# Seven products in place of eight: a second Strassen stage in a fused FNet and SwiGLU kernel on Trainium2

## The chip, the cores and the metric

The kernel runs on one core of one Trainium2 chip, in one launch. The metric is the device time of that launch in microseconds (us), as a median of several executions. The profile shows one further execution. Five engines matter here: TensorE (PE in the profile, PEld for its weight loads), VectorE (DVE), ScalarE (ACT), GpSimd (POOL) and SyncE (SP). In this kernel SP and POOL mostly issue transfers (DMAs).

## The reference

The input is x, 2048 tokens of 512 numbers, fp32. A condition vector gives six modulation vectors; between them stand two sublayers, a Fourier mixing and a gated feed-forward of width F = 1792.

```python
mod = (_silu(c) @ w_mod).reshape(c.shape[0], 6, 1, -1)
sa, ca, ga, sb, cb, gb = (mod[:, 0], mod[:, 1], mod[:, 2], mod[:, 3], mod[:, 4], mod[:, 5])
h = _layernorm(x) * (1 + ca) + sa
a = jnp.einsum("bsd,ed->bse", h, dft_hid_re)
b = jnp.einsum("bsd,ed->bse", h, dft_hid_im)
y = jnp.einsum("ts,bse->bte", dft_seq_re, a) - jnp.einsum("ts,bse->bte", dft_seq_im, b)
x = x + ga * y
h = _layernorm(x) * (1 + cb) + sb
gate, up = h @ w1, h @ w3          # 512 -> 1792, twice
x = x + gb * ((_silu(gate) * up) @ w2)   # 1792 -> 512
```

## The kernel before

**Tiles.** A tile has 128 partitions. Tokens lie in four blocks t of 512, the 512 features in four chunks d of 128, and F in seven groups g of 256, each of two chunks q of 128. Big tiles come from 50 slots of [128, 2, 512] fp32, handed out first in, first out (`take`, `give`). A slot that is taken again makes the new writer wait for the last readers of the old tile. PSUM has eight banks of [128, 512] fp32.

**Precision.** Every fp32 product is three matmul passes in a faster format (`product`, L98 to L106): high part by high part, high by low, low by high. ScalarE makes the high part of an operand by a copy (`copy`, L87), VectorE the low part by a subtraction (`minus`, L90). So each operand of TensorE costs these two engines one pass each, the low after the high.

**Stages.** First come the norm, its modulation and the DFT over features; then the DFT over the sequence (`seq_unit`, L750); then the second norm (`ln2`), whose first blocks 0 and 2 begin when half of the sequence products are done; then the feed-forward. The feed-forward works on two pairs of token blocks, PAIRS = ((0, 2), (1, 3)). For the first pair the groups g = 0 and 1 are plain: `up_block` forms gate and up of one block and chunk in 12 matmuls each, `down_unit` one product with w2 in 6. Then come 12 *items*, each a group g and a pair: g = 2 to 6 of the first pair, then g = 0 to 6 of the second. `turning` = 5 is the first item of the second pair.

**An item.** Its products with w1 are the units a1 to a7, those with w3 the units b1 to b7 (`factor`). They are the seven products of Strassen's method (in Winograd's form) over a 2 x 2 split of the weights and of the operand, whose other side is the two token blocks. A unit is 6 matmuls. Their sums are built with copies by ScalarE (n = 1, 5, 6) and additions by VectorE (n = 2, 3, 7); `result` then puts silu on the w1 side and multiplies with the w3 side, which gives h, a tile v; its high and low part are `hf`. The products with w2 are 8 second products y for a pair (two blocks by four feature chunks), 6 matmuls each, so an item has 14 + 8 = 22 units. They run one item late: those of an item stand among the units of the next. ScalarE copies each result from the bank, scaled by gb (`copy_by`, L335); after two of them GpSimd issues a transfer that adds the y tile (512 KB) to `sums[t, i]` in DRAM (L1146). For the second pair and g = 5 and 6, VectorE adds into SBUF instead (`own`).

**What sets the order.** Each engine runs its own instructions in the order in which the program writes them. The units' order is the string `body` with `head` in the main loop; a minus sign marks units of the item before. Beside the units runs work from two queues, `background` (modulation columns, residual additions, second norm) and `jobs` (weights): `advance` takes steps from them while there is credit of VectorE and ScalarE time, with a rule for free slots, and stops at a `PAUSE`. `behind(n, fn)` puts a piece of work n units later. The steps of a weight (`weight_jobs`) are: high parts, four sums over its quarters, low parts, and high and low parts of the sums.

**Other parts that the change touches.** `mod_columns` forms the modulation vectors ga, sb, cb and gb: w_mod's columns by silu(c) (`times`), then two `tensor_reduce`. `add_sums` adds the last quarter of the sequence products to the blocks 1 and 3 (VectorE, L808); these steps stand at the end of `background`. `judge` forms a flag from sums of squares that were taken on the way, with which the kernel tells whether its shortcuts hold for the DFT matrices given; some 15 small operations of VectorE. The flag chooses at the very end between ending and another program (`general`), which doesn't run here.

Of the kernel before, what the change touches and what calls it, by code (L numbers as in the profile page):

```python
# [15 lines left out]
P = 128  # L16
# [26 lines left out]
def folded(nc, pools, c, cp, wmr, wmc, x, xt, ctr, cti, wdr, wdi, w1, w3, w2, out):  # L43
# [300 lines left out]
    def mod_columns(v, dst):  # L344
        w = {}

        def fetch(i):
            w[i] = take(F32, "wmc")
            nc.sync.dma_start(w[i], wmc[v, i])

        def scale(i):
            times(w[i], w[i], sc_row[0][:, 0, :].unsqueeze(1).to_broadcast([P, 2, N]))

        def total(i):
            r1 = small.tile([P, 32], F32, name=f"r1_{v}_{i}", tag="r1")
            nc.vector.tensor_reduce(
                out=r1,
                in_=flat(w[i]).rearrange("p (a b) -> p a b", b=32),
                axis=AX.X,
                op=OP.add,  # L360
            )
            nc.vector.tensor_reduce(
                out=dst[:, 2 * i : 2 * i + 2],
                in_=r1.rearrange("p (a b) -> p a b", b=16),
                axis=AX.X,
                op=OP.add,
            )
            give(w[i])
# [12 lines left out]
        background.extend([PAUSE] * 2)  # L381
        for i in range(2):
            step(background, 0, lambda i=i: scale(i), 1.2)
            step(background, 0, lambda i=i: total(i), 1.3)
        step(background, 0, end, 0.1)
# [689 lines left out]

    def up_block(g, t, q, w):
        if q == 0 and w == "w1":
            drain(lambda: ("h2", t, 1) in done)
        to = bank(turn[0] % 4)
        turn[0] += 1  # L1080
        for d in range(ND):
            at = slice(d * P, (d + 1) * P)
            product(
                to,
                [u[:, q, at] for u in wuse[w, g]],
                [u[t, d // 2][:, d % 2, :] for u in (h2h, h2l)],
                d == 0,
                d == ND - 1,
            )
        if t == PAIRS[0][1] and q == 1:  # L1090
            give_w((w, g))
# [117 lines left out]
    state, vs = {}, {}  # L1209

    def right(pair, n):
        t0, t1 = PAIRS[pair]
# [6 lines left out]
    def result(i, w, q, k, src):  # L1219
# [16 lines left out]
        behind(1, highs)  # L1236
        behind(2, lows)

    def factor(i, w, n):
# [37 lines left out]
        if n == 3:  # L1277
# [3 lines left out]
            if w == "w3":  # L1281
                for x in vs.pop(i):
                    behind(3, lambda x=x: give(x))

# [269 lines left out]
    give(zz)  # L1554

    USED = {"w1": (0.0, 0.5), "w3": (1.2, 0.5), "y": (0.0, 0.6), "own": (0.7, 0.0)}
# [6 lines left out]

    def beside(us, used):
        advance(us - used[0], us - used[1], jobs)
        if not jobs:
            advance(0.0, 0.0)

    def up(g, t):
        for q in range(2):
            for w in ("w1", "w3"):
                drain(lambda: ((w, g), "l") in done, jobs)
                delayed()
                up_block(g, t, q, w)
                beside(2.72, USED[w])

    def down(g, pair, t, d, key):
        drain(lambda: (key, "l") in done, jobs)  # L1580
        delayed()
        down_unit(g, pair, t, d, key)
        beside(1.36, USED["own" if pair == 1 and g >= NG - 2 else "y"])
# [36 lines left out]

    def unit(kind, i, n):
        g, pair = items[i]
# [13 lines left out]
        if (kind, n) == ("a", 6):  # L1636
            load_w(("w2", g, pair))
        if (kind, n) == ("a", 3) and more:
            load_w(("w3", *items[i + 1]))
            weight_jobs(i + 1, "w1")  # L1640
        if (kind, n) == ("b", 2):
            plain_jobs(("w2", g, pair))
        if (kind, n) == ("b", 3):
# [5 lines left out]
            if i + 1 == turning:  # L1649
                other_operands()  # L1650
            if more:
                weight_jobs(i + 1, "w3")
            for t in PAIRS[pair]:
                seconds.extend((g, pair, t, d, ("w2", g, pair)) for d in range(ND))
        beside(1.36, FACTOR[kind][n])

    weight_jobs(0, "w3")
    ln2(1)
    ln2(3)
    for i in range(len(items)):  # L1660
        body = "a6 a5 y a7 y y a4 y a3 y b1 y b2 y b6 b5 y"
        if i == turning:
            body = "y y y y y a6 y a5 y a7 y b1 b2 a4 b6 a3 b5"
        if i == len(items) - 1:
            body = "a6 a5 y a7 y y a4 y a3 b1 y b2 b6 b5 y b7 y b4 y b3 y y y y y y y y"
        head = "-b7 a1 -b4 -b3 a2 " if i == turning else "-b7 a1 a2 -b4 -b3 " if i else "a1 a2 "
        for at in (head + body).split():
            if at == "y":
# [3 lines left out]
            elif at[0] == "-":  # L1672
                unit(at[1], i - 1, int(at[2]))
            else:
                unit(at[0], i, int(at[1]))
    while later:
# [803 lines left out]
```

## Time and profile before

| | |
|---|---|
| time, median of 3 runs | 710.24 us (709.85 to 710.78) |
| profiled execution, its own time | 708.46 us |
| its span from the first to the last instruction | 706.7 us |
| mean granted TensorE clock | 0.991 |
| sequence products | 88 to 262 us |
| plain groups of the first pair, with the second norm | 262 to about 320 us |
| items of the first pair, then of the second | to about 503 us, then to the end |
| HBM read, written | 76.81 MB, 33.55 MB |

The page gives busy times per engine over the whole span, so a share there is a mean over stages with different limits. Groups of instructions stand as line, engine, operation, destination <- source with their shapes, count, busy time and mean ns; an idle time in brackets is what the engine waited just before an instruction, and for whom. TensorE's matmuls are pipelined: one lasts about 390 ns, and they start about 230 ns apart.

### The profile page before, as it was taken

The numbers are of one execution on the slowest core, as the hardware profiler recorded it, in microseconds if no ns is written. First come the engines' busy times: TensorE is split into PE (matmuls) and PEld (weight loads), VectorE is DVE, ScalarE is ACT, GpSimd is POOL, SyncE is SP. The second block draws the span as 40 slices with busy tenths as digits, with TensorE's granted clock in tenths as the row PEclk, the third lists the DMA queues.
The fourth block names the chain that finished last, engine by engine and source line by source line (L and its number), as shares of the span: only waits on it lengthen the run. The fifth ranks groups of instructions, "written<-read, shape, count | busy, mean of one in ns | idle before, by whom it ended". The sixth has DMA issues, their size and how long they took to land.

```text
span 706.7 us, 8912 instructions
## 1 busy us (share of the span) xinstructions
PE 686.3 (97%) x3152; PEld 564.7 (80%) x3152; DVE 548.3 (78%) x877; ACT 430.8 (61%) x709; POOL 119.4 (17%) x141
## 2 busy tenths in 40 slices
PE   7999999999999999899999999999999999999995
PEld 4898888888888888687888788787788888888784
DVE  5999679997999978579987886896865556664763
ACT  4998865545454655745677676867665565656420
POOL 1320253542524000200100101011010100101000
PEclk9999999999999999999999999999999999999998
DMA  8730299796678521522868558376763847537403
GB/s 266 211 120 1 77 373 328 251 307 229 207 283 287 168 86 41 92 58 64 209 114 199 89 130 153 61 156 137 239 136 73 180 62 175 111 69 162 137 0 124
DMA packets 38100, 108.93 MB, mean 154 GB/s; under 512 B 4896, under 2 KB 5152, under 8 KB 38048
## 3 DMA queue, kind: packets, MB, share of 16 engines
q0 software_dynamic: 12352, 43.00, 29.3%
q1 hardware_dynamic: 25264, 63.98, 27.5%
q10 hardware_dynamic: 432, 1.31, 0.5%
q8 instruction: 26, 0.43, 0.3%
q14 instruction: 26, 0.21, 0.1%
HBM read 76.81 MB, written 33.55 MB: 156 GB/s over the span
## 4 chain that ended last, share of the span: by engine, by line
PE 81%; DVE 7%; ACT 6%; issue 2%; DMA 2%; SPq 1%; ACTq 0%; DVEq 0%
PE bank L100 52%; PE bank L750 25%; PE bank L559 2%; PE bank L598 1%; DMA wmr<-in_wmr 1%; ACT xc L894 1%; PE bank L576 1%; DVE xc L96 1%; SPq L231 1%; ACT hf L87 1%; ACT y L335 1%; DVE v L96 0%; DVE hl L90 0%; ACT hm L501 0%; DMA w<-in_wdi 0%
## 5 line engine op out<-in xcount | busy, mean ns | idle before, releaser
L100 PE MATMUL bank<-hf,w2h 128*128 128x512 f32 (+1 forms) x452 | 140.9, 391 | 0.3
L1146 POOL DMA_DIRECT2D sum<-y x48 | 41.0, 855 | 390.1 <-ACT y L335 373.0
L100 PEld LDWEIGHTS bank<-hf,w2h 128*128 128x128 f32 x452 | 84.3, 188 | 22.1 <-DVE hf L90 3.4
L100 PE MATMUL bank<-hf,w2l 128*128 128x512 f32 (+1 forms) x226 | 87.6, 388 | 0.0
L87 ACT ACTIVATE hf<-v 128x512 fp32r<-128x512 f32 x56 | 35.3, 630 | 67.3 <-DVE v L96 62.7
L335 ACT ACTIVATE y<-bank,gb 128x512 f32<-128x512 f32 x96 | 64.9, 682 | 18.6 <-PE bank L100 18.3
L93 DVE TENSOR_TENSOR v<-bank,x 128x512 f32<-128x512 f32 x36 | 24.7, 685 | 34.9 <-PE bank L100 34.8
L750 PE MATMUL bank<-bh,us 128*128 128x512 f32 x128 | 49.9, 390 | 0.0
L93 DVE TENSOR_TENSOR x<-bank,x 128x512 f32<-128x512 f32 x36 | 24.7, 687 | 32.4 <-PE bank L100 28.7
L750 PE MATMUL bank<-bh,ul 128*128 128x512 f32 x128 | 49.8, 389 | 0.0
L750 PE MATMUL bank<-d,us 128*128 128x512 f32 x128 | 49.8, 389 | 0.0
L750 PE MATMUL bank<-d,uh 128*128 128x512 f32 x128 | 49.8, 389 | 0.0
L750 PE MATMUL bank<-l,us 128*128 128x512 f32 x128 | 49.8, 389 | 0.0
L750 PE MATMUL bank<-l,uh 128*128 128x512 f32 x128 | 49.8, 389 | 0.0
L100 PEld LDWEIGHTS bank<-hf,w2l 128*128 128x128 f32 x226 | 42.4, 188 | 8.4
L90 DVE TENSOR_TENSOR hf<-v,hf 128x512 fp32r<-128x512 f32 x56 | 38.5, 687 | 12.2 <-ACT hf L87 12.1
L170 POOL DMA_INDIRECT re<-in_ctr,mirror x32 | 35.8, 1117 | 66.2 <-DVE ul L90 39.5
L1224 ACT ACTIVATE v<-v 128x512 f32<-128x512 f32 x36 | 22.8, 632 | 38.8 <-DVE v L93 38.8
L87 ACT ACTIVATE x<-bank 128x512 f32<-128x512 f32 x72 | 41.4, 586 | 7.2 <-PE bank L100 6.5
L170 POOL DMA_INDIRECT im<-in_cti,mirror x32 | 32.7, 1023 | 35.3 <-PE bank L750 10.0
L100 PE MATMUL bank<-h2h,w1h 128*128 128x512 f32 x80 | 31.8, 397 | 1.5 <-ACT h2h L87 1.5
L100 PE MATMUL bank<-h2l,w1h 128*128 128x512 f32 x80 | 31.9, 399 | 0.8 <-DVE h2l L90 0.8
(246 smaller groups left out, 1775.2 us busy)
## 6 DMA issues: line engine op xcount, KB each, us to landing
sum<-y POOLq DMA_DIRECT2D x48, 512.0 KB, 5.6
w<-in_w SPq DMA_DIRECT2D x42, 512.0 KB, 4.5
re<-in_ctr SPq DMA_DIRECT2D x32, 256.0 KB, 5.0
im<-in_cti SPq DMA_DIRECT2D x32, 256.0 KB, 5.0
wmc<-in_wmc SPq DMA_DIRECT2D x8, 512.0 KB, 6.3
xr<-in_xt SPq DMA_DIRECT2D x8, 512.0 KB, 7.6
sum<-xr SPq DMA_DIRECT2D x8, 512.0 KB, 6.2
x<-in_x SPq DMA_DIRECT2D x11, 256.0 KB, 4.8
```

Source lines behind the costliest of these rows:

```text
L87: nc.scalar.activation(dst, src, AF.Copy, scale=scale)
L90: nc.vector.tensor_tensor(out=dst, in0=a, in1=b, op=OP.subtract)
L93: nc.vector.tensor_tensor(out=dst, in0=a, in1=b, op=OP.add)
L96: nc.vector.tensor_tensor(out=dst, in0=a, in1=b, op=OP.mult)
L100: nc.tensor.matmul(acc, lhs[a], rhs[b], start=first and n == 0, stop=last and n == len(PASSES) - 1, skip_group_check=more,)
L170: nc.gpsimd.indirect_dma_start(dst, None, rows, bass.IndirectOffsetOnAxis(ap=at, axis=0))
L231: queue.dma_start(raw_w[dt][q * 64 : (q + 1) * 64, m, :], w[i][par::2, q])
L335: nc.scalar.activation(dst, src, AF.Identity, scale=by)
L559: nc.tensor.matmul(halves(hb[k])[:, m, :], sides((hh, hl)[a][k])[:, dt, m, :], wu[dt][:, b, m, :], start=False, stop=dt % 2 == 1 and n == ...
L750: nc.tensor.matmul(acc[what, e], lhs, rhs, start=begin and i == 0, stop=(end or (turn and what == "x")) and i == len(terms) - 1, skip_grou ...
L1146: nc.gpsimd.dma_start(sums[t, d // 2], y, accum_op=OP.add)
L1224: behind(k != 0 or q == 0, lambda: nc.scalar.activation(v, src, AF.Silu))
```

## The change

The second products of the second pair's items with g = 0 to 4 (`SEVEN`, five items) become seven products M1 to M7 each in place of eight. The split is 2 x 2 over the two chunks q of h and the two token blocks on one side, and over the quarters of w2 on the other. VectorE forms four combinations of h's quarters and of w2's; these and their high and low parts are new operands (`seven_parts`, `seven_jobs`). The products run in the order 2, 5, 3, 1, 6, 7, 4, each on both banks 6 and 7 (two output chunks, 3 + 3 matmuls). M2, M5 and M1 begin new banks; the others add to what the banks hold (M3 to M5's, M6, M7 and M4 to M1's). After each product ScalarE copies both banks, which stay held, and GpSimd adds the y tile to `sums` of one block and half; the sums come out right because each output block gets copies of the partial sums that belong to it. So there are seven accumulating transfers an item in place of four.

```diff
+    SEVEN = [(g, 1) for g in range(NG - 2)]
+    ORDER7 = (2, 5, 3, 1, 6, 7, 4)
+    LEFT7 = {1: "h0", 2: "h2", 4: "h3", 5: "s0", 6: "s1", 7: "s2", 3: "s3"}
+    TO7 = {2: (0, 0), 5: (1, 1), 3: (0, 1), 1: (0, 0), 6: (0, 1), 7: (1, 1), 4: (1, 0)}
...
         times(v, v, src)
+        if (g, pair) in SEVEN:
+            seven_parts(i, q, k)
+            return
...
+    def seven_parts(i, q, k):
...
+        if (q, k) != (0, 1):
+            n = {(0, 0): 1, (1, 0): 2, (1, 1): 3}[q, k]
+            behind(1, lambda: high(n, v[q, k]))
+            behind(2, lambda: low(n, v[q, k]))
+            return
+        t1, t2, t3, t4 = v[0, 0], v[1, 1], v[0, 1], v[1, 0]
+        behind(1, lambda: minus(t1, v[0, 1], v[0, 0]))
+        behind(2, lambda: high(5, t1))
+        behind(2, lambda: minus(t3, v[1, 1], v[0, 1]))
+        behind(3, lambda: low(5, t1))
+        behind(3, lambda: minus(t2, v[1, 1], t1))
+        behind(4, lambda: high(7, t3))
+        behind(4, lambda: minus(t4, v[1, 0], t2))
+        behind(5, lambda: high(6, t2))
+        behind(5, lambda: low(7, t3))
+        behind(6, lambda: high(4, t4))
+        behind(7, lambda: low(6, t2))
+        behind(8, lambda: low(4, t4))
...
+    def seven_unit(g, pair, n, key):
+        new = n in (1, 2, 5)
+        if new:
+            banks7[:] = [bank(6), bank(7)]
+        y = take(F32, "y")
...
+        for e, to in enumerate(banks7):
+            at = int(LEFT7[n][1]) * HALF + e * P
+            product(
...
+            copy_by(y[:, e, :], to, gb[:, d : d + 1])
+        give(u)
+        nc.gpsimd.dma_start(sums[t, which], y, accum_op=OP.add)
+        behind(4, lambda: give(y))
```

`seven_jobs` has the five steps of `weight_jobs`, for w2. The order of units after such an item changes, ScalarE gets no step from the queues in a unit ahead of a y (`hold`), and the next item's w3 steps are queued at b6 in place of b3:

```diff
+        if i and items[i - 1] in SEVEN:
+            body = "a6 a5 a7 y a4 y a3 y b1 y b2 y b6 y b5 y"
...
-    def beside(us, used):
-        advance(us - used[0], us - used[1], jobs)
+    def beside(us, used, hold=False):
+        if hold:
+            credit[1] = min(credit[1], 0.0)
+        advance(us - used[0], 0.0 if hold else us - used[1], jobs)
...
+            hold = after == "y" and i > 0 and items[i - 1] in SEVEN
```

Around it five other edits stand. The last six background steps (additions to the blocks 1 and 3) move into the last four pauses of the second norm's last block of the first pair. `ln2(1)` and `ln2(3)` are queued earlier, and the check's sums later, at the third item of the second pair:

```diff
+    def fill_pauses():
+        last = [background.pop() for _ in range(6)][::-1]
+        fillers = [last[:1], last[1:3], last[3:4], last[4:]]
+        at = len(background)
+        while fillers:
+            at -= 1
+            if background[at][-1] is None:
+                for slots, _, _, fn in fillers.pop()[::-1]:
+                    background.insert(at, (slots, 0.0, 0.0, fn))
...
-    judge()
+    ln2(1)
+    ln2(3)
     up(0, 2)
...
-    ln2(1)
-    ln2(3)
     for i in range(len(items)):
+        if i == turning + 2:
+            judge()
```

A plain up block is written in two parts of six matmuls with steps from the queues between (`up_block(g, t, q, w, part)`, `beside(1.36, ...)` after each). And the modulation columns use one operation per 128 columns that multiplies and sums:

```diff
-        def scale(i):
-            times(w[i], w[i], sc_row[0][:, 0, :].unsqueeze(1).to_broadcast([P, 2, N]))
-
-        def total(i):
...
+        def total(i, b):
+            sums, junk = parts[i], w[i][:, b, :]
+            for n in range(ND):
+                nc.vector.scalar_tensor_tensor(
+                    junk[:, cols(n)],
+                    junk[:, cols(n)],
+                    1.0,
+                    sc_row[0][:, 0, cols(n)],
+                    op0=OP.mult,
+                    op1=OP.mult,
+                    accum_out=sums[:, b, n : n + 1],
+                )
```

More of the change, by code (lines that the diff above doesn't have):

```diff
@@ L349, in fetch @@
             nc.sync.dma_start(w[i], wmc[v, i])
-        def scale(i):
-            times(w[i], w[i], sc_row[0][:, 0, :].unsqueeze(1).to_broadcast([P, 2, N]))
-        def total(i):
[L355 to L368, printed above, removed]
+        def total(i, b):
[10 more added lines that the diff above has]
+                )
+            if b:
+                nc.vector.tensor_reduce(
+                    out=dst[:, 2 * i : 2 * i + 2], in_=sums, axis=AX.X, op=OP.add
+                )
+                give(w[i])
+        parts = [
+            small.tile([P, 2, ND], F32, name=f"r1_{v}_{i}", tag="r1") for i in range(2)
+        ]
         def end():
@@ new lines, in seven_jobs, with highs, totals, lows @@
+    def seven_jobs(key):
+        use = wuse[key] = {}
+        def highs():
+            use["h"] = take(F32R, "w2h")
+            copy(flat(use["h"]), flat(wraw[key]))
+        def totals():
+            use["s"] = take(F32, "w2s")
+            s, r = four(use["s"]), four(wraw[key])
+            plus(s[:, 0, :], r[:, 1, :], r[:, 3, :])
+            minus(s[:, 1, :], s[:, 0, :], r[:, 0, :])
+            minus(s[:, 2, :], r[:, 0, :], r[:, 1, :])
+            minus(s[:, 3, :], r[:, 2, :], s[:, 1, :])
+        def lows():
+            use["l"] = take(F32R, "w2l")
+            r = wraw.pop(key)
+            minus(flat(use["l"]), flat(r), flat(use["h"]).bitcast(F32))
+            give(r)
+        def sum_highs():
+            use["sh"] = take(F32R, "w2sh")
+            copy(flat(use["sh"]), flat(use["s"]))
+        def sum_lows():
+            use["sl"] = take(F32R, "w2sl")
+            minus(flat(use["sl"]), flat(use["s"]), flat(use["sh"]).bitcast(F32))
+            give(use.pop("s"))
+            done.add((key, "l"))
+        step(jobs, 1, highs, 0.0, 1.0)
+        step(jobs, 1, totals, 1.4)
+        step(jobs, 1, lows, 1.2)
+        step(jobs, 1, sum_highs, 0.0, 1.0)
+        step(jobs, 1, sum_lows, 1.2)
```

89 lines of the change are left out of this document (67 added, 22 removed).

## The prediction

> **What bounds the kernel now.** The page comes first: how busy each engine is, and which engines lie on the chain that ended last.
>
> ```profile
> PE 686.3 (97%) x3152; PEld 564.7 (80%) x3152; DVE 548.3 (78%) x877; ACT 430.8 (61%) x709; POOL 119.4 (17%) x141
> PE 81%; DVE 7%; ACT 6%; issue 2%; DMA 2%; SPq 1%; ACTq 0%; DVEq 0%
> ```
>
> TensorE is the bound. The chain of waits, in order of time (start, us, what), gives its pace in two long stretches without a pause:
>
> ```profile
> 88.22 174.32 PE bank L750 x768
> 503.44 156.17 PE bank L100 x682
> ```
>
> 174.32/768 is 227 ns a matmul in the sequence stage, 156.17/682 is 229 ns in the second pair. I call six matmuls a unit: 6 x 228.5 ns = 1.37 us. The change is mostly in the second pair, so I ask the busy times of one of its items (span, busy us and instructions of PE, PEld, DVE, ACT and POOL, granted clock, DMA share, GB/s), and when GpSimd issues the same sum in two neighbouring items (start, us, engine):
>
> ```profile
> 542.17:572.34 30.17, 30.17 (x134) 24.70 (x132) 17.85 (x28) 18.24 (x28) 3.40 (x4) 1.00 0.60 122
> 517.30 0.85 POOL L1146 DMA_DIRECT2D sum<-y  x1 [22.17 <-ACT y L335]
> 547.46 0.85 POOL L1146 DMA_DIRECT2D sum<-y  x1 [13.46 <-ACT y L335]
> ```
>
> An item lasts 547.46 - 517.30 = 30.16 us, which is its 22 units (22 x 1.371 = 30.16): TensorE never waits there, and VectorE and ScalarE are idle 40% of the time. What the change gives TensorE is a gain only if these two keep up in their new order.
>
> **The second products: what goes.** 42 matmuls take the place of 48 in five items: 5 x 6 x 228.5 ns = 6.85 us less for TensorE; an item would last 21 x 1.371 = 28.79 us.
>
> **What comes.** The groups of the second pair (busy, mean ns) have every new operation's size:
>
> ```profile
> L335 ACT ACTIVATE y<-bank,gb 128x512 f32<-128x512 f32 x40 | 27.4, 684 | 10.4 <-PE bank L100 10.3
> L87 ACT ACTIVATE x<-bank 128x512 f32<-128x512 f32 x30 | 17.6, 585 | 3.9 <-PE bank L100 3.9
> L90 DVE TENSOR_TENSOR hf<-v,hf 128x512 fp32r<-128x512 f32 x20 | 13.7, 686 | 3.5 <-ACT hf L87 3.5
> L87 ACT ACTIVATE hf<-v 128x512 fp32r<-128x512 f32 x20 | 12.7, 633 | 23.3 <-DVE v L96 21.5 <-issue 1.3 <-ACT w3h L87 0.6
> L96 DVE TENSOR_TENSOR v<-v,x 128x512 f32<-128x512 f32 x15 | 10.4, 693 | 0.5
> L93 DVE TENSOR_TENSOR x<-bank,x 128x512 f32<-128x512 f32 x15 | 10.4, 692 | 26.6 <-PE bank L100 22.9 <-ACT y L335 3.6
> L90 DVE TENSOR_TENSOR w1sl<-w1s,w1sh 128x1024 fp32r<-128x1024 f32 x5 | 6.1, 1225 | 0.0
> L87 ACT ACTIVATE w1sh<-w1s 128x1024 fp32r<-128x1024 f32 x5 | 5.3, 1063 | 0.6
> ```
>
> Queued behind each other, VectorE's instructions start closer together than they last (start, us):
>
> ```profile
> 542.37 1.22 DVE L90 TENSOR_TENSOR w3l<-w,w3h 128x1024 fp32r<-128x1024 f32 x1
> 543.51 0.68 DVE L90 TENSOR_TENSOR hf<-v,hf 128x512 fp32r<-128x512 f32 x1
> 544.11 1.22 DVE L90 TENSOR_TENSOR w3sl<-w3s,w3sh 128x1024 fp32r<-128x1024 f32 x1
> 552.06 0.41 DVE L93 TENSOR_TENSOR w1s<-w 128x256 f32<-128x256 f32 x1
> 553.53 1.22 DVE L90 TENSOR_TENSOR w1l<-w,w1h 128x1024 fp32r<-128x1024 f32 x1
> ```
>
> So 1.14 us for 1024 columns, 0.60 for 512 (0.7 when it needs the one before), 1.47 for the four of a weight's sums. VectorE gets three more lows and four differences (7 x 0.6), w2's sums (1.47) and their low (1.14): 6.8 us more an item. ScalarE gets six more y copies, three highs and w2sh: 6 x 0.6 + 3 x 0.55 + 1 = 6.3 us. Both go to about 24.6 of 28.8 us. The sum of busy time still fits; the order decides. Two places do not fit.
>
> *The held copies.* ScalarE in a middle item of the second pair, from the copies of the fourth second product (M1) to those of the sixth (M7); bank6 and bank7 are the banks of the second products, hf_850 the high part of an item's first h. Now, then before at the same place:
>
> ```order
> L335 ACTIVATE y_846_5323<-bank6_844_5321,gb_152 128x512
> L335 ACTIVATE y_846_5323<-bank7_845_5322,gb_152 128x512
> L87 ACTIVATE w1sh_847_5333<-w1s_840_5305 128x1024
> L87 ACTIVATE hf_850_5346<-v_816_5171 128x512
> L335 ACTIVATE y_851_5348<-bank6_844_5321,gb_152 128x512
> L335 ACTIVATE y_851_5348<-bank7_845_5322,gb_152 128x512
> L87 ACTIVATE w2h_852_5358<-w2_824_5218 128x1024
> ```
>
> ```order
> L335 ACTIVATE y_820_5190<-bank6_821_5191,gb_152 128x512
> L87 ACTIVATE w1sh_823_5201<-w1s_819_5184 128x1024
> L87 ACTIVATE x_825_5210<-bank3_824_5203 128x512
> L335 ACTIVATE y_820_5190<-bank7_827_5214,gb_152 128x512
> L87 ACTIVATE w2h_829_5232<-w2_805_5104 128x1024
> L87 ACTIVATE hf_831_5236<-v_797_5055 128x512
> ```
>
> Before, each y was read from a bank that TensorE needs again only two products later. Now bank6_844 is read, added to and read again, so M7's matmuls wait for the copies of M6, and these stand behind hf_850. VectorE's order at that place:
>
> ```order
> L90 TENSOR_TENSOR w1sl_848_5335<-w1s_840_5305,w1sh_847_5333 128x1024
> L93 TENSOR_TENSOR x_842_5317<-bank4_849_5337,x_842_5317 128x512
> L96 TENSOR_TENSOR v_816_5171<-v_816_5171,x_842_5317 128x512
> L93 TENSOR_TENSOR w2s_853_5360<-w2_824_5218 128x256
> L90 TENSOR_TENSOR w2s_853_5360<-w2s_853_5360,w2_824_5218 128x256
> ```
>
> hf_850 needs v_816, which stands behind w1sl_848, which needs w1sh_847, which stands behind both copies of M1. The chain from the start of M1: its second bank is done after 1.37 + 0.16 (a matmul lasts 389 ns, the pace is 229) = 1.53; then y 0.68, w1sh 1.06, w1sl 1.22, x 0.69, v 0.69, hf 0.63, first copy of M6 0.68: 7.2 us. TensorE has M1, one factor, M6, one factor: 4 x 1.371 = 5.5 us. It waits 1.7 us for M7 at least. w1h and an x copy stand ahead of M1's copies and make them about 0.2 late: I take 1.9, bounds 1.6 and 2.2.
>
> *VectorE's stretch at the head of an item.* From b7's sum to the sum that a7 needs it does 13 operations of 512 columns (8.3 us), the w3 sums (1.47) and two lows of 1024 (2.3): 12.05 us with nothing to wait for. Its start is 1.53 us into b7's unit; the next user of a7's bank is a4, nine units (12.34 us) after b7's start. 1.53 + 12.05 - 12.34: TensorE waits 1.3 us, between 0 (a few rows shorter) and 2.0. Before, this stretch had no differences and no extra lows.
>
> Item: 28.79 + 1.9 + 1.3 = 32.0 us, 1.83 us above 30.16; five items give **+9.1 us**, bounds +1.2 (1.6 and 0) and +14 (2.2 and 2.0).
>
> *The check's sums* stand in the second such item at the head of that stretch:
>
> ```profile
> 299.70 0.42 DVE L1006 TENSOR_REDUCE sq<-chk 128x8 f32<-128x256 f32 x1 [0.27 <-POOL sq L1005]
> 302.66 0.14 DVE L1026 TENSOR_SCALAR bad<-fine 1x1 int32<-1x1 f32 x1
> ```
>
> 302.80 - 299.70 = 3.1 us of VectorE, 0.3 of which it would idle for b7: **+2.8 us**, 0 if the stretch had slack.
>
> **The second norm.** Before, TensorE pauses when the third token block's operands come late (start, us):
>
> ```profile
> 262.38 0.39 PE L100 MATMUL bank<-h2h,w1h 128*128 128x512 f32 x1
> 294.80 0.39 PE L100 MATMUL bank<-hf,w2l 128*128 128x512 f32 x1
> 296.71 0.51 PE L100 MATMUL bank<-h2h,w1h 128*128 128x512 f32 x1 [1.53 <-ACT h2h L87]
> 297.97 0.79 PE L100 MATMUL bank<-h2l,w1h 128*128 128x512 f32 x1 [0.76 <-DVE h2l L90]
> ...
> 301.03 0.39 PE L100 MATMUL bank<-h2h,w1l 128*128 128x512 f32 x1
> ```
>
> From 294.80 to 301.03 nine matmuls start (2.06 us at the full pace): 4.2 us lost, 1.5 of it because the seven from 297.97 on are 0.44 us apart, about half pace. With the norm further on at that time the operands are there, and this goes. But VectorE now does the additions ahead of the product that the down units need (v_377, hf_379). Now, then before:
>
> ```order
> L96 TENSOR_TENSOR xc_342_2546<-xc_342_2546,stat_341_2538 128x1024
> L808 SCALAR_TENSOR_TENSOR xr_328_2382<-sum_348_2605,ga_148,xr_328_2382 128x512 x2
> L96 TENSOR_TENSOR xc_350_2616<-xc_350_2616,stat_341_2538 128x1024
> L808 SCALAR_TENSOR_TENSOR xr_297_2106<-sum_348_2605,ga_148,xr_297_2106 128x512 x2
> L96 TENSOR_TENSOR v_377_2781<-v_377_2781,bank3_378_2786 128x512
> L90 TENSOR_TENSOR hf_379_2805<-v_377_2781,hf_379_2805 128x512
> ```
>
> ```order
> L840 TENSOR_REDUCE s_2_377_2721<-q_2_377_2716 32x16
> L96 TENSOR_TENSOR v_377_2714<-v_377_2714,bank3_378_2723 128x512
> L90 TENSOR_TENSOR hf_379_2737<-v_377_2714,hf_379_2737 128x512
> L883 RECIPROCAL s_2_377_2721<-s_2_377_2721 32x16
> ```
>
> The products moved behind the norm's multiplies and four additions. Durations there:
>
> ```profile
> 273.53 0.69 DVE L96 TENSOR_TENSOR v<-v,bank 128x512 f32<-128x512 f32 x1 [1.15 <-PE bank L100]
> 276.68 2.00 ACT L87 ACTIVATE w2h<-w 128x1024 fp32r<-128x1024 f32 x2
> 277.76 2.36 DVE L90 TENSOR_TENSOR w2l<-w,w2h 128x1024 fp32r<-128x1024 f32 x2 [1.80 <-ACT w2h L87]
> 285.78 1.28 ACT L880 ACT_TABLE_LOAD   x1
> 287.08 0.31 ACT L880 ACTIVATE s<-s,eps 32x16 f32<-32x16 f32 x1
> 287.69 0.70 DVE L847 COPY w<-s 32x16 f32<-32x16 f32 x4
> 289.18 2.36 DVE L96 TENSOR_TENSOR xc<-xc,stat 128x1024 f32<-128x1024 f32 x2
> 290.49 1.53 ACT L894 ACTIVATE xc<-xc,sb,cb 128x512 f32<-128x512 f32 x2 [1.37 <-issue]
> ```
>
> The second block's product ends about 275.5 (274.2 before, and two additions ahead of it). ScalarE then does hf 0.63, a table load 1.28, the root 0.31, a table load back 1.28, the gate 0.6, w2h 1.0: 280.6. VectorE: two lows 2.36, inverse and spread 1.65 (copies 0.70 with the small ones on either side), product and low 2.0, then multiply 1.2, additions 1.4, multiply 1.2, additions 1.4, v_377 0.69: 292.5. ScalarE: hf 0.63, two modulations 1.53, and only then the first y copy 0.62: 295.3. The fifth down unit needs that bank at 262.38 + 8 x 2.74 + 4 x 1.37 = 289.8 (eight up units of twelve matmuls and four down units). A wait of 5.5 us, and half pace after it as before (1.5): 7.0 against 4.2 lost is **+2.8 us** (-4.2, where the wait vanishes, to +4.5: parts of this queue may run ahead of what I walk through, or behind).
>
> The half pace followed pauses of 1.53 and 0.76 us, little more than 2 us without work; a wait of 1.9 us in an item may therefore cost up to 1.5 us of clock as well, five times 1.5 = 7.5 us (rival three); smaller waits in the first pair did not. The Trainium skill (TensorE: Matmul & The Clock Gate, in the section Part 1: The HAM clock gate) lets the clock fall only after at least one idle window of about 3.4 us. By that rule the items' waits cost no clock and the sum stays as it is; the rows above disagree with it.
>
> **The rest.** In the first pair the waits of TensorE, from 300 to 510 us (in all, times, longest), are mostly these:
>
> ```profile
> PE bank L100 <- ACT x L87: 1.2, 3, 0.5
> PE bank L100 <- DVE v L93: 0.3, 1, 0.3
> ```
>
> 1.5 us. The norm of blocks 1 and 3 starts some 25 us earlier there and the check's sums are out of the way, so I take **-1.5** (to +3, as the same pauses may recur in other units). The halves of the first up products only let background work in twice as often. The reload of the four sums goes out on SP after the last M4; the products that add to them come 7 to 10 units (9.6 to 13.7 us) later, which hides it, and an excess over that would be lost once. GpSimd issues 7 sums an item at 0.85 us, 6 of 32 us, and the check's memset: nothing.
>
> The modulation columns' products and sums go from 2.4 us to eight multiply-adds of 128 columns on VectorE; TensorE runs unbroken there, so nothing either way. Sum: 9.1 + 2.8 + 2.8 - 1.5 = +13.2 us. The profiled execution took 708.46 (span 706.7), so it would take 721.7; the runs' median is 710.24, 1.8 above it, so runs at **723.4**.
>
> **Rivals.** One: faster. If M1-to-M7 takes under 5.5 us and VectorE's stretch under 10.8, the items keep all 6.85 us, and the norm's 4.2 go: 710.2 - 11.1 = 699.1 (to 706 with half of it). For it: both engines fit in sum. Against: the chain's seven rows, none of which can shrink by a quarter. Chance 0.10. Two: only the least waits (1.6 an item), the check hidden and the norm no worse than now: +1.2, 711.4, from 707 (the norm's 4.2 gone) to 714; chance 0.14, of which 0.04 faster and 0.05 within 0.2%. Three: the clock falls at each item's wait: 7.5 more, 731 (729 to 735); chance 0.09. Four: the transfers.
>
> ```profile
> q0 software_dynamic: 576, 2.10, 43.6%
> q1 hardware_dynamic: 432, 1.57, 14.2%
> ```
>
> In 542 to 573 us four sums took 43.6% of 31 us, 3.4 us each; seven and the weights make 23.7 + 4.4 = 28 of 32 us. They fit while items last that long; if slots come free late, an item of 34 gives 733. Chance 0.04. The forecast, 715 to 730, has 0.63.
>
> **Numbers.** A measurement can tell 0.2%, 1.4 us. Faster 0.14 (rival one and 0.04 of two), same 0.05, slower 0.81. The range 710 to 732 leaves out rival one (0.10), four (0.04), a third of three (0.03) and the low end of two (0.03): 0.2.
>
> **What would show it.** After: items of about 32 us between like sums on GpSimd; waits of TensorE on ScalarE's y, near 1.9 us, five times; on VectorE's v near 1.3; one wait of some 5 us in the down units before the third token block. Items of 29 us or no such waits make it wrong.

## The result, and the profile after

The changed kernel takes 734.27 us (median of 6 runs, 732.60 to 736.96) beside 709.75 us before (708.49 to 710.78): 1.035 times as long, 95% interval 1.0325 to 1.0372. I had forecast slower, but 723.4 us and at most 732: of 24.5 us I had found 13.2. The profiled execution took 732.60 us, its span 730.7, 24.0 more than before.

The first row of the page, busy times, shows where to look: TensorE is as busy as before (686.7 against 686.3 us) although it runs 30 matmuls fewer in the record. What came is therefore waiting, and matmuls at a lower clock.

```profile
PE 686.7 (94%) x3122; PEld 560.9 (77%) x3122; DVE 578.0 (79%) x1049; ACT 457.4 (63%) x759; POOL 134.1 (18%) x156
```

TensorE's waits in the second pair, from 500 to 720 us (waited for: us in total, times, longest). Of before, from 500 to 700 us, this list has one entry, of 0.2 us:

```profile
PE bank L100 <- ACT y L335: 9.0, 5, 1.8
PE bank L100 <- DVE v L93: 4.7, 5, 1.0
PE bank L100 <- ACT x L87: 2.2, 4, 1.7
PE bank L100 <- DVE x L93: 1.8, 1, 1.8
```

Five waits for y (1.8 us each) and five for v (0.9 to 1.0): one of each for every item with seven products, as forecast. The waits for x are of the check's sums and of a smaller wait that comes below. The chain behind the wait for y, from M1's copies to M7, in the fourth of these items (rows of ScalarE, VectorE and TensorE, put in order of time):

```profile
599.66 1.28 ACT L335 ACTIVATE y<-bank,gb 128x512 f32<-128x512 f32 x2
600.80 1.08 ACT L87 ACTIVATE w1sh<-w1s 128x1024 fp32r<-128x1024 f32 x1
601.92 1.23 DVE L90 TENSOR_TENSOR w1sl<-w1s,w1sh 128x1024 fp32r<-128x1024 f32 x1 [1.37 <-ACT w1sh L87]
603.06 0.68 DVE L93 TENSOR_TENSOR x<-bank,x 128x512 f32<-128x512 f32 x1
603.78 0.69 DVE L96 TENSOR_TENSOR v<-v,x 128x512 f32<-128x512 f32 x1
604.50 0.63 ACT L87 ACTIVATE hf<-v 128x512 fp32r<-128x512 f32 x1 [2.62 <-DVE v L96]
605.04 1.25 ACT L335 ACTIVATE y<-bank,gb 128x512 f32<-128x512 f32 x2
605.76 0.50 PE L100 MATMUL bank<-hf,w2sh 128*128 128x512 f32 x1 [1.81 <-ACT y L335]
```

Each instruction is released by the one above it, because it reads its result or stands behind it in the same queue; ScalarE stands idle for 2.62 us in the middle, with M6's copies queued behind `hf`. TensorE's last matmul started at 603.56, so it lost 605.76 - 603.56 - 0.23 = 1.97 us. I had taken 1.9.

What I had given a chance of 0.09 is in the next rows, three pairs of neighbouring stretches of 3.41 us (TensorE's busy time and matmuls stand second, the granted clock third from the end):

```profile
569.74:573.16 3.42, 1.62 (x8) 1.13 (x7) 2.78 (x7) 2.60 (x4) 0.52 (x1) 1.00 0.74 145
573.16:576.57 3.41, 3.41 (x10) 2.63 (x9) 1.89 (x2) 3.06 (x6) 1.18 (x2) 0.50 0.80 119
638.01:641.42 3.41, 1.73 (x7) 1.42 (x8) 2.64 (x7) 2.98 (x5) 0.85 (x1) 1.00 0.59 113
641.42:644.84 3.42, 3.42 (x17) 2.81 (x16) 2.06 (x2) 3.42 (x7) 0.85 (x1) 1.00 0.92 140
668.73:672.14 3.41, 1.60 (x8) 1.02 (x6) 1.99 (x3) 1.36 (x3) 0.00 (x0) 1.00 1.05 196
672.14:675.56 3.42, 3.42 (x15) 2.82 (x16) 1.83 (x2) 3.42 (x6) 0.96 (x2) 1.00 0.51 66
```

Behind M7's wait at 571 us the clock is at half for 3.41 us, which costs 1.7; behind those at 639 and 671 us it is not. In this run three of the five items lost such a stretch. GpSimd's first sum of an item comes every 37.6, 33.9, 33.9 and 32.3 us (521.92, 559.53, 593.48, 627.41, 659.75): 32.3 without the clock, 33.9 with it, 37.6 with the check's sums too.

In the second norm the wait before the fifth down unit is there, at its forecast size (TensorE, then ScalarE):

```profile
289.85 0.39 PE L100 MATMUL bank<-hf,w2l 128*128 128x512 f32 x1
295.33 1.22 PE L100 MATMUL bank<-hf,w2h 128*128 128x512 f32 x2 [5.09 <-ACT y L335]
292.66 0.63 ACT L87 ACTIVATE hf<-v 128x512 fp32r<-128x512 f32 x1 [2.79 <-DVE v L96]
293.20 1.50 ACT L897 ACTIVATE xc<-xc,sb,cb 128x512 f32<-128x512 f32 x2
294.61 1.24 ACT L335 ACTIVATE y<-bank,gb 128x512 f32<-128x512 f32 x2
```

From 289.85 to 295.33 are 5.48 us; less the usual 0.23 that is 5.25 us lost, where I had 5.5. What follows calls everything up to the end of the first pair the front. By the start of the same instructions, the first Strassen product and a plain product with w1 at the end of the first pair:

```profile
324.11 0.50 PE L100 MATMUL bank<-th,w1sh 128*128 128x512 f32 x1 [0.23 <-ACT x L87]
329.24 0.50 PE L100 MATMUL bank<-th,w1sh 128*128 128x512 f32 x1 [1.48 <-ACT x L87]
503.44 0.50 PE L100 MATMUL bank<-h2h,w1l 128*128 128x512 f32 x1 [0.21 <-DVE w1l L90]
508.24 0.39 PE L100 MATMUL bank<-h2h,w1l 128*128 128x512 f32 x1
```

The first and third row are of before, the others of after: 5.1 us are lost ahead of the items and 4.8 by the end of the first pair; the other 19.2 (24.0 - 4.8) come in the second pair.

### The profile page after: what moved, and what is told of

It reads as the page before. It is cut to its first block, busy times and chain, and to the rows that moved or that the text cites. A ratio compares the mean times of both kernels' runs of the same rounds, so it can differ in the third digit from the quotient of the medians.

```text
span 730.7 us, 9127 instructions
## 1 busy us (share of the span) xinstructions
PE 686.7 (94%) x3122; PEld 560.9 (77%) x3122; DVE 578.0 (79%) x1049; ACT 457.4 (63%) x759; POOL 134.1 (18%) x156
## 5 line engine op out<-in xcount | busy, mean ns | idle before, releaser
L100 PE MATMUL bank<-hf,w2h 128*128 128x512 f32 (+1 forms) x352 | 112.0, 399 | 5.4 <-ACT y L335 5.1
L87 ACT ACTIVATE hf<-v 128x512 fp32r<-128x512 f32 x71 | 44.8, 630 | 90.8 <-DVE v L96 78.2
L335 ACT ACTIVATE y<-bank,gb 128x512 f32<-128x512 f32 x126 | 82.2, 686 | 12.5 <-PE bank L100 12.4
L100 PEld LDWEIGHTS bank<-hf,w2h 128*128 128x128 f32 x352 | 67.4, 193 | 23.1 <-ACT y L335 6.5
L1153 POOL DMA_DIRECT2D sum<-y x28 | 24.0, 857 | 251.5 <-ACT y L335 236.2
L100 PE MATMUL bank<-hf,w2l 128*128 128x512 f32 (+1 forms) x176 | 68.9, 391 | 0.0
L90 DVE TENSOR_TENSOR hf<-v,hf 128x512 fp32r<-128x512 f32 x71 | 48.8, 688 | 18.9 <-ACT hf L87 18.9
L1345 POOL DMA_DIRECT2D sum<-y x35 | 29.8, 852 | 148.0 <-ACT y L335 145.0
L170 POOL DMA_INDIRECT im<-in_cti,mirror x32 | 36.1, 1127 | 29.9 <-issue 11.9
L100 PEld LDWEIGHTS bank<-hf,w2l 128*128 128x128 f32 x176 | 34.0, 193 | 7.0
L100 PE MATMUL bank<-hf,w2sh 128*128 128x512 f32 x80 | 25.3, 397 | 9.0 <-ACT y L335 9.0
```

The costliest lines, as they stand in the source:

```text
L87: nc.scalar.activation(dst, src, AF.Copy, scale=scale)
L90: nc.vector.tensor_tensor(out=dst, in0=a, in1=b, op=OP.subtract)
L100: nc.tensor.matmul(acc, lhs[a], rhs[b], start=first and n == 0, stop=last and n == len(PASSES) - 1, skip_group_check=more,)
L170: nc.gpsimd.indirect_dma_start(dst, None, rows, bass.IndirectOffsetOnAxis(ap=at, axis=0))
L335: nc.scalar.activation(dst, src, AF.Identity, scale=by)
L1153: nc.gpsimd.dma_start(sums[t, d // 2], y, accum_op=OP.add)
```

## Experiments on the items

Every ratio below is to the kernel before, run on the same chip at the same time.

**The seven products alone, and all but them.** `SEVEN = []` in the changed kernel, and the changed kernel with its five other edits undone:

> The changed kernel with all second products plain (eight for every item), the other five edits kept. Theory (the items' second products cost some 19 us through the M6/M7 chain, VectorE's stretch and the clock; the rest some 5): 714 to 717 us, with the norm's wait of about 5 us before the fifth down unit and its half clock still there, and no wait over 0.5 us in the items except for the check's sums. Rival (the rest is harmless by itself and all 24 us come from the items): 709 to 711. Rival (the norm and the early start of blocks 1 and 3 cost more than seen): over 719.

> The kernel before with the seven products alone: additions, second norm, check's sums, whole up blocks and modulation columns as before. Theory: 709.75 - 6.85 + five times (2.0 at M7 + 1.1 at a4 + 0.4 at a7, and 0.3 of slow starts) + 1.7 for each of 3 to 5 half-clock windows = 725 to 730 us. If the items' losses needed the other edits (the check's sums alone, or slots that come free later), it is at 703 to 712.

Measured: without the seven products 717.27 us beside 708.66, ratio 1.013 (1.009 to 1.016), above the forecast; alone 723.75, ratio 1.023 (1.018 to 1.029), a little below. The products bring some 15 to 17 us, the rest some 9. Alone, they show the same five waits for y of 1.8 us and five for v of up to 1.0 in the trace, so neither the check's sums nor the edits to the front make them.

**M1's operand one unit later.** This takes `hf` out of the chain:

```diff
-            behind(1, lambda: high(n, v[q, k]))
-            behind(2, lambda: low(n, v[q, k]))
+            behind(1 + (n == 1), lambda: high(n, v[q, k]))
+            behind(2 + (n == 1), lambda: low(n, v[q, k]))
```

> The changed kernel with one thing moved: the high part of M1's right operand (and its low part) one unit later, so that ScalarE copies M6 out of its banks ahead of it. Theory (chain M1 copies, w1sh, w1sl, x, v, hf, M6 copies): M7's wait of 2.0 us goes in all five items, and with it the half-clock windows behind it: 734.3 - 10.4 - 5 to 8.5 = 715 to 719 us, clock 0.99. Rival (the wait is ScalarE's or the transfers' load and moves elsewhere): 729 to 735. Rival (the clock falls for another reason): 723 to 725 with half windows still in the items.

Measured: 719.43 us, less than the changed kernel by 14.8 us by the medians and by 13 by the ratios (1.0163 for 1.0348). The waits for v and y in the second pair, 500 to 730 us:

```profile
PE bank L100 <- DVE v L93: 4.7, 5, 1.0
PE bank L100 <- ACT y L335: 1.8, 1, 1.8
```

Four of five are gone (the fifth stands in an item to which the edit doesn't reach), and no stretch of half clock is left in the items. 4 x 2.08 us (the 1.97, and 0.11 because the second matmul behind a wait starts 0.34 us after the first and not 0.23) are 8.3. The rest, some 5 to 6 us, goes with the three stretches of half clock, 3 x 1.7 = 5.1 us in the changed kernel's trace. So this edit shows the wait and what the clock makes of it.

**The same without the other edits, and in all five places; then a3 ahead of a4.** The second moves the product that needs VectorE's sum of a7 two units back, and with it two lines for the weights (when w1's are given back and w3's loaded):

```diff
-            body = "a6 a5 a7 y a4 y a3 y b1 y b2 y b6 y b5 y"
+            body = "a6 a5 a7 y a3 y a4 y b1 y b2 y b6 y b5 y"
```

> The kernel before with the seven products alone, and the high part of M1's operand one unit later (in the last such place too). Theory: 723.75 - 5 x 2.08 at M7 - 3.4 to 8.5 of half clock = 706 to 710 us: no more than the price of the waits at a4 and a7 is then left, which eats the 6.85 us. Rival (something else in the seven products costs): over 713.

> As the one with M1's operand later, and in the same items a3 ahead of a4, so that the product that needs VectorE's sum of a7 comes two units (2.7 us) later. Theory (VectorE's stretch from b7 to a7 is 1.1 us too long for its place, and only for its place): the wait at a4 goes in five items, 5 x 1.3 = 6.5 us: 700 to 703 us, faster than before. Rival (VectorE is full, so the wait comes back behind it): 706 to 710.

Measured: 709.27 us, ratio 0.9996 (0.9982 to 1.0010), as expected: gain and a4's waits cancel. And 709.28, ratio 0.9994: the rival's time came, though not for its reason. The wait at a4 had gone, and M5 waited in its place, for M2's copies (ScalarE, then TensorE):

```profile
576.05 0.63 ACT L1234 ACTIVATE v<-v 128x512 f32<-128x512 f32 x1 [0.96 <-DVE v L93]
576.58 1.25 ACT L335 ACTIVATE y<-bank,gb 128x512 f32<-128x512 f32 x2
577.31 0.50 PE L100 MATMUL bank<-hf,w2sh 128*128 128x512 f32 x1 [0.80 <-ACT y L335]
```

The copies stand behind the silu of a7, which waits 0.96 us for VectorE's sum. If only ScalarE's order is in the way and not VectorE's load, the next edit must take the wait away.

**ScalarE's silu and M2's operand later.**

```diff
-            behind(k != 0 or q == 0, lambda: nc.scalar.activation(v, src, AF.Silu))
+            late = k == 1 and i > 0 and items[i - 1] in SEVEN
+            behind(2 if late else k != 0 or q == 0, lambda: nc.scalar.activation(v, src, AF.Silu))
...
+            wait = {1: (2, 3), 2: (3, 3), 3: (1, 2)}[n]
+            behind(wait[0], lambda: high(n, v[q, k]))
+            behind(wait[1], lambda: low(n, v[q, k]))
```

> The kernel before with the seven products, M1's operand later, a3 ahead of a4, and now ScalarE's silu of a7 and a3 and M2's operand one or two units later, behind the copies of M2's banks and of a6. Theory (each remaining wait is one ScalarE step that stands ahead of a copy which TensorE waits for): no wait over 0.3 us in the five items, which then last 28.8 to 29 us, 700 to 703 us. Rival (the wait moves once more, since VectorE's stretch is full): 706 to 710.

Measured: 702.78 us beside 710.34, ratio 0.989 (0.9875 to 0.9909). The list of TensorE's waits from 500 us on is empty. So VectorE was not full, and the seven products gain what they were worth on paper (6.85 us) as soon as nothing that waits for VectorE stands ahead of a copy that TensorE waits for.

## Experiments on the other edits

**The check's sums back in the norm.**

> The changed kernel with the check's sums where they stood before (behind the first down units). Theory: the two waits of 2.0 and 1.9 us in the third item of the second pair become 0 and 0.3, worth 3.5 us; in the norm VectorE has no work for most of 3 us there while it waits for ScalarE's copies, so at most 1 is given back: 730 to 732 us. Rival (VectorE's stretch binds there all the same): 734.

Measured: 732.94 us (731.41 to 737.01), no difference that can be told. The two waits in the third item went, but behind the norm the first Strassen product then waited 4.5 us for ScalarE's x (1.5 in the changed kernel), with 6.8 us of half clock behind it. In the item the sums cost 37.61 - 33.95, some 3.7 us, where I had 2.8. The changed kernel's trace shows why (GpSimd, then VectorE):

```profile
541.23 0.85 POOL L1345 DMA_DIRECT2D sum<-y  x1 [2.75 <-ACT y L335]
541.77 0.51 POOL L1008 MEMSET sq<- 128x96 f32 x1
542.32 0.42 DVE L1009 TENSOR_REDUCE sq<-chk 128x8 f32<-128x256 f32 x1 [2.77 <-POOL sq L1008]
545.35 0.69 DVE L93 TENSOR_TENSOR x<-bank,x 128x512 f32<-128x512 f32 x1
```

VectorE waits for the memset, which stands behind GpSimd's sum, which waits for ScalarE. I had called the memset nothing.

**Additions and early norm, each alone in the kernel before.**

> The kernel before with one edit: the additions to blocks 1 and 3 in the last pauses of the second norm (eight second products everywhere, all else as before). Theory (the additions push the fifth down unit's product and the modulations ahead of its y copy): a wait of about 5 us before the fifth down unit and two half-clock windows behind it, 7.6 us lost where 4.2 were, and nothing given back later: 711 to 713 us beside some 709 for before. Rival (the additions were in somebody's way where they stood before): 705 to 708.

> The kernel before with one edit: the second norm of blocks 1 and 3 queued before the third block's up units in place of before the items. Theory (VectorE is then busy without a break between 305 and 330 us, so the first item's copy and sums come late): 1 to 3 us slower, 710 to 712 us. Rival (what I had forecast, norm earlier and waits of the first pair gone): 707 to 708.

Measured: 709.10, ratio 0.9990 (0.9978 to 1.0003), and 709.51, ratio 0.9995 (0.9984 to 1.0007). Neither loses anything; both my theories fell. The additions, which I had blamed for the wait before the fifth down unit, don't make it by themselves: the longest wait for y there is 0.4 us.

**The halves of the up blocks:** alone, with the additions, and everything but them (all three with eight second products).

> The kernel before with one edit: the plain up blocks in two parts with background work between. Theory (the halves let the second norm's steps in twice as often, so root, inverse and modulations stand ahead of the down units' y copies, and the additions no longer matter): the wait before the fifth down unit appears here, 2 to 5 us slower, 711 to 715. Rival (only halves and additions together do it): 708 to 710, or 1 to 3 faster, since the norm is ready earlier.

> The kernel before with two edits: halves of the up blocks and additions in the pauses. Theory: the y copy stands behind product and modulations, wait of about 5 us and two half-clock windows, 3 to 4 us slower than before: 712 to 714 us. If it is at 709, the early norm of blocks 1 and 3 is needed as well.

> The changed kernel with eight second products everywhere and whole up blocks; additions in the pauses, early second norm, late check's sums and new modulation columns kept. Theory (the split is needed for the loss in the norm): no wait for y before the fifth down unit; some 710 to 712 us, of which 2 are the check's sums in the third item of the second pair. Rival (additions or early norm lose by themselves beside the late check's sums): 715 to 718 as with the split.

Measured: 711.97, ratio 1.0026 (1.0007 to 1.0044); 709.40, 0.9985 (0.9972 to 0.9997); and 706.49 beside 710.34, 0.994 (0.9918 to 0.9960), faster than before. Against the 1.013 of the same kernel with halves, they cost 13 us there by the ratios, 11 by the medians. Alone and with the additions they cost 1.6 or nothing: it takes the other edits as well.

TensorE's waits for y from 262 to 690 us, with the halves alone and then with the additions too; the longest is the one before the fifth down unit:

```profile
PE bank L100 <- ACT y L335: 2.2, 2, 1.8
PE bank L100 <- ACT y L335: 4.9, 2, 4.4
```

So the halves open this wait, and beside them the additions lengthen it from 1.8 to 4.4 us, by the order that the prediction showed: VectorE does them ahead of the product that the down units need. The kernel with both is none the slower for it; in its trace the pauses of the kernel before, which cost 4.2 us, are gone.

The halves undone in the changed kernel itself:

```diff
                 for part in range(2):
                     up_block(g, t, q, w, part)
-                    beside(1.36, USED[w] if part else (0.0, 0.0))
+                beside(2.72, USED[w])
```

> The changed kernel with one edit undone: the plain up blocks whole again, with background work only behind each. Theory (the halves, together with additions, early second norm and late check's sums, cost some 10 us between 262 and 510 us, seen as 717.3 against 706.5 with eight second products): 734.3 - 10 = 722 to 726 us, no wait over 1 us for y before the fifth down unit. Rival (with the seven products the front loses the same without the halves): 732 to 735.

Measured: 723.31 us, 11.0 less. ScalarE around the fifth down unit, and the same two instants as above:

```profile
285.76 0.31 ACT L883 ACTIVATE s<-s,eps 32x16 f32<-32x16 f32 x1
289.27 0.67 ACT L335 ACTIVATE y<-bank,gb 128x512 f32<-128x512 f32 x1
289.93 1.52 ACT L897 ACTIVATE xc<-xc,sb,cb 128x512 f32<-128x512 f32 x2
...
321.90 0.39 PE L100 MATMUL bank<-th,w1sh 128*128 128x512 f32 x1
...
497.64 0.39 PE L100 MATMUL bank<-h2h,w1l 128*128 128x512 f32 x1
```

The root of the norm comes at 285.76 (277.96 with halves: twice as many chances for background work), and the first y copy at 289.27, now ahead of the modulations and not behind. The first product comes 7.3 us earlier than with halves, the end of the first pair 10.6. The traces differ by up to 4.5 us in when the plain products begin (first product with w1 at 261.5 to 266.1 us), so the stretch from there is the safer measure: to the same product at the end of the first pair it takes 241.1 us before, 245.4 in the changed kernel and 234.4 here, which makes 11.0 for the halves.

**What is left of the front.** Eight second products, whole up blocks, and the check's sums at b6 of the last item but one with the memset ahead of the items; then the same with the old modulation columns; with those and the late norm; and the check's sums alone:

> Eight second products everywhere, whole up blocks, additions in the pauses, early second norm, new modulation columns, and the check's sums at b6 of the last item but one with their memset early. Theory (what is left of the loss with the late check's sums is VectorE's wait for the memset behind the transfers on GpSimd, and 3 us at the head of an item): 2 us less than with the check's sums in the third item of the second pair: 704 to 706 us. Rival (the check's sums cost the same there): 706 to 708.

> The front with eight second products everywhere, whole up blocks, additions in the pauses, early second norm and late check's sums, but the modulation columns as before. Theory (the columns are worth nothing either way, as I had forecast): as with the new columns, 703 to 705 us. Rival (the columns bring the front forward): 706 to 708.

> The kernel before with two edits, additions in the pauses and late check's sums; second norm of blocks 1 and 3 queued late as before, old columns, whole up blocks. Theory (the early norm gives the waits of the first pair's items, some 3 us, the two edits here the rest): 706 to 708 us. Rival (without the early norm nothing is gained): 709 to 710.

> The kernel before with the check's sums alone moved to b6 of the last item but one, their memset ahead of the items. Theory (VectorE binds between 300 and 330 us, and the 3.1 us of the check's sums there are what the front gains): 1 to 3 us faster, 707 to 709 beside 710. Rival (they cost nothing where they stood; the gain needs the norm to be earlier): 709.5 to 710.5.

Measured: 703.47, ratio 0.992 (0.9892 to 0.9945); 708.46, 0.998 (0.9966 to 0.9990); 708.87, 0.997 (0.9959 to 0.9987); 710.10, 0.9999 (0.9989 to 1.0010). The front alone came out below its forecast. The columns, which I had put at nothing, are worth some 4 us beside the others by the ratios and 5.3 by the stretch just used (234.3 us with the new ones, 239.6 with the old); the check's sums alone and the early norm add nothing that can be told. With old columns the stretch takes 239.9 us with halves and additions, so that the halves seem to cost 11 us only beside the new columns; no two runs differ in that alone. How the columns look on VectorE, new ones first (the front alone), then old ones:

```profile
111.18 0.31 DVE L354 SCALAR_TENSOR_TENSOR wmc<-wmc,scr 128x128 f32<-128x128 f32 x1
111.43 0.28 DVE L354 SCALAR_TENSOR_TENSOR wmc<-wmc,scr 128x128 f32<-128x128 f32 x1
111.64 0.28 DVE L354 SCALAR_TENSOR_TENSOR wmc<-wmc,scr 128x128 f32<-128x128 f32 x1
L354 DVE SCALAR_TENSOR_TENSOR wmc<-wmc,scr x64: 280/285/314, 111.2 to 182.0; 128x128 f32<-128x128 f32 x64
...
110.18 1.25 DVE L96 TENSOR_TENSOR wmc<-wmc,scr 128x1024 f32<-128x1024 f32 x1
111.46 1.22 DVE L356 TENSOR_REDUCE r<-wmc 128x32 f32<-128x1024 f32 x1
112.72 0.19 DVE L362 TENSOR_REDUCE ga<-r 128x2 f32<-128x32 f32 x1
L356 DVE TENSOR_REDUCE r<-wmc x8: 1219/1221/1221, 111.5 to 187.6; 128x32 f32<-128x1024 f32 x8
```

The new ones start 0.21 us apart, so eight take 1.7 us and a small reduction, where the old pair with its reduction took 112.82 - 110.18 = 2.6 (the next instruction started at 112.82). The last starts at 182.0 rather than 187.6; the norm stands behind the columns in the same queue, and its root came at 287.36 rather than 289.99. That this order carries the gain is read from the traces, not tried apart.

**All together:** the changed kernel with whole up blocks, the four moves of order (M1's and M2's operands, a3 ahead of a4, the silu), and the check's sums in that late place:

```diff
+        if (kind, i, n) == ("b", len(items) - 2, 6):
+            judge()
...
-        if i == turning + 2:
-            judge()
```

> The changed kernel with whole up blocks, the four moves in the items' order (M1's and M2's operands, a3 ahead of a4, ScalarE's silu later) and the check's sums at b6 of the last item but one, their memset ahead of the items. Theory: the items give their 6.85 us, the front some 4 to 6 as with eight products: 696 to 699 us. Rival (the two gains are the same VectorE time and don't add): 701 to 704.

Measured: 696.53 us beside 709.51, ratio 0.983 (0.981 to 0.986), the fastest of all. One of its items, as busy times:

```profile
575.33:604.24 28.91, 28.88 (x128) 23.60 (x127) 24.45 (x39) 23.71 (x38) 5.97 (x7) 1.00 0.89 184
```

28.9 us with TensorE busy throughout; VectorE at 24.5 and ScalarE at 23.7 us, which the prediction had at 24.6 each, do fit. Nor are the transfers in the way, my fourth rival: with all seven sums an item the DMA engines are busy for 0.89 of this one, and TensorE doesn't wait. It beats the front alone by 6.9 us (703.47 - 696.53), which is the price of the five units fewer.

## Why the prediction was wrong

Two steps failed. The sum left out the clock behind the waits in the items, which took 5.1 us, and it put the halves of the up products at nothing, which beside the other edits cost 11 us. The second is partly hidden in the total, because the columns, also put at nothing, gained 4 to 5 us: that the front came out only some 3.5 us above its forecast is luck.

*The second products and their load.* Right: -6.85 us, and the two engines' sums.

*The held copies and VectorE's stretch.* Right in mechanism and size: 1.97 us for 1.9 at M7, 1.1 to 1.2 for 1.3 at a4. Missed was a third wait, 0.3 us at a7 (0.4 with the slow start behind it, in four items), where ScalarE's copy of a6 stands behind an `hf`: some 1.7 us in all. The experiment with a3 ahead of a4 shows that behind the wait at a4 stood another, in ScalarE's order, which my list didn't have.

*Clock.* Wrong, and the largest gap between the sum and the trace of the second pair: I gave the half clock a chance of 0.09, and kept it out of the sum. Three stretches at 1.7 us are 5.1. I had the row for it (half pace behind pauses of 1.53 and 0.76 us) and reasoned it down. The Trainium skill (TensorE: Matmul & The Clock Gate, in Part 1: The HAM clock gate), which I had quoted for the fall after at least one idle window of 3.4 us, also states that the window is free-running. This agrees: within a run all such stretches start on one grid (573.16 and 607.29 are 10 x 3.413 apart), and between 85 and 690 us they last 3.41 us or twice that. That a whole idle window is needed does not agree: 1.80 us of idle in a window sufficed.

*The check's sums.* Mechanism right, 3.7 for 2.8: VectorE waited for the memset, which I had called nothing, because of its place in GpSimd's queue.

*The second norm.* The size of the wait was right (5.25 for 5.5, from the order of the instructions), its cause only half right. I read the additions as what stood in front. The runs show that the halves bring the norm's steps there; without halves the additions cost nothing, with them they lengthen the wait (1.8 to 4.4 us). "The halves of the first up products only let background work in twice as often" was a term at zero. It is worth 11 us, since without the halves the same edits gained. What beside the halves it takes is not shown. Half the clock followed for 4.8 us rather than 3.4, so the norm cost 4.6 by the first product (with the next term's wait) and not 2.8.

*The first pair.* -1.5 forecast, about 0 came: the waits recurred, as the first one shows (1.48 us for x, where 0.23 was). And the columns at nothing: wrong by 4 to 5 us; that it is because their steps stand ahead of the norm in one queue is the likely reason, not a tried one.

By the same instants: front +4.8 (0.5 of it ahead of the first plain product, which is less than that instant varies between traces) for +1.3; second pair +19.2 for +11.9. That is 7.3 us more; the clock (5.1), the wait at a7 (1.7) and the check's sums (0.9) make 7.7 of it, which is as near as these sums come.

## What to carry to other kernels

When a bank is read and then added to again, its copy becomes part of TensorE's path: look at each instruction ahead of that copy in its engine's queue, and at what it waits for. A change that only lets other work in more often moves everything behind it in program order; follow the queue to the first instruction that TensorE waits for before costing it at nothing. And a wait that is taken away may show the next one at once: the one at a4 came back at M5, and only both together gave the gain.

## What the runs showed of the hardware

A wait of TensorE of about 1.8 us can cost 1.7 us more in clock, or nothing, by where it falls in a fixed raster of windows of 3.41 us. Idle time here is the time in a window between the end of one matmul and the start of the next, over all twenty profiles of this case, from 85 to 690 us and in windows at full clock. Windows with up to 1.75 us of it were never followed by half clock, the twelve with over 2.1 us always, and of nineteen with 1.78 to 1.81 us fifteen were.

In the other four the wait reaches an edge of its window or crosses it, or, as the one at 671 us, ends only 0.1 us ahead of it. Of the fifteen, two held two waits; the other thirteen held one that lay within both edges and ended at least 0.24 us ahead of the second. Why the edge counts stays open, and since the ends of matmuls are modelled in these profiles, the distances are rough.

The six runs of the changed kernel lie 4.4 us apart at granted clocks of 0.981 to 0.986, before's 2.3 us apart. That the number of such stretches in a run makes this spread is likely, but only one of the six has a trace.
